# Four low halves of weights from GpSimd to VectorE, and a check of limits as six separate steps

## Chip, cores and metric

One core of one Trainium2 chip runs the whole program. The metric is the device time in microseconds (us) of one execution, the median of several runs.

## What is computed

The reference is a gated linear attention over 4 x 8 heads of 768 steps, followed by a mixture of eight experts with the best two chosen for each token, followed by a dense MLP:

```python
for t in range(S):                                   # attention
    state = alpha[:, :, t, :, None] * state + einsum('bhd,bhe->bhde', k[:, :, t], v[:, :, t])
    y[:, :, t] = einsum('bhd,bhde->bhe', q[:, :, t], state)
x = y.transpose(0, 2, 1, 3).reshape(3072, 384)
z = x @ w_gate + log1p(exp(x @ w_noise)) * noise     # 3072 x 8
top2 = two largest of z per row; weights = softmax of the two
out[tokens of e] += weight * (maximum(x[tokens of e] @ w1[e], 0) @ w2[e])      # 384 -> 1024 -> 384
h = out @ w_in;  result = maximum(0.01 * h, h) @ w_out                         # 384 -> 2048 -> 384
```

## The kernel before

Attention runs in 24 units of 128 tokens (build_unit). The tokens of four units form a tile; for each tile a chain of small VectorE operations (gate_top2 and build_route) picks the two experts and gives every choice a slot, and GpSimd scatters the rows into slots in DRAM with an indirect DMA (L1267, 48 scatters in all). Then the experts run (build_experts): each group is one expert's rows, 320 to 512 of them, and for each 128 of the 1024 hidden columns, a step, there is a first product of 9 matmuls into the PSUM tile ph (gemm1, L751), the high half hh on ScalarE (L769), the low half on VectorE into the same tile (L779), and a second product into py (gemm2, L799 and L795). There are two ph buffers, so a first product waits for the VectorE low half of two steps before. The second product of a step stands two steps behind (LAG = 2). Expert 0's first 320 rows are the first group, begun as the last attention units finish.

Products are made of high and low halves, three matmuls for one. Weights come in pairs of 128-column blocks, four pairs per expert, so pair j serves steps 2j and 2j+1. For each pair w1 and w2 are loaded into staging tiles w1s and w2s (two buffers each, L495 and L498), ScalarE writes the high half (split_hi, L504), and split_lo (L508) subtracts it from the staged tile to give the low half, 128 x 768, after which the staging tile is free for the next load. For expert 0 all eight low halves are on GpSimd, for expert 1 on VectorE, for the others on either.

The order on each engine is written by a planner (class Planner) when the program is built: every step has an estimated duration, what it depends on, rings of buffers, and a due time worked back from those who need it. Among the steps that can start first on an engine, it takes the one with the earliest due time. Steps marked port=True on VectorE and GpSimd are planned one after another. The engines then run their lists in that order, whatever the real times. Scatters are planned at least 1.7 us apart.

The slots were laid out with fixed sizes, so raise_flag checks, once the counts are known, that no limit was broken; if one was, a general path recomputes everything at the end. flag_sums puts the 19 sums on all partitions with small matmuls into the PSUM tile pA, and raise_flag, a single step of the plan with 3.0 us, compares them on VectorE in 18 small instructions (L635 to L652), several of which multiply one SBUF column by another.

Of the kernel before, what the change touches and what calls it, by code (L numbers as in the profile page):

```python
# [7 lines left out]
FT = mybir.dt.float32  # L8
# [5 lines left out]
OP = mybir.AluOpType  # L14
AX = mybir.AxisListType
# [11 lines left out]
SIZES = ((320, 512),) + ((384, 448),) * 7  # L27
G0 = 384
EARLY = 2
# [6 lines left out]
CAP = sum(SIZES[0])  # L36
SURE, CLEARED = 656, 4
# [4 lines left out]
BIG = 1.0e30  # L42
# [38 lines left out]
class Planner:  # L81
# [8 lines left out]
    def add(self, eng, dur, fn, deps=(), use=(), takes=(), phase=1, due=1e9, lat=0.0, size=0, own=1e9, port=False, room=None, rows=0):  # L90

        deps = list(deps)
        st = Step(eng, dur, fn, deps, list(takes), phase, due, lat, size)
        st.port, st.room, st.rows = port, room, rows
        st.own = own
        for owner, ring in use:
            deps.append(owner)
            owner.holders[ring].append(st)
        for ring in st.takes:
            ring.planned.append(st)  # L100
        self.steps.append(st)
        return st
# [271 lines left out]
def tile_kernel(  # L374
# [21 lines left out]
    nc = tc.nc  # L396
    B, H, S, D = q.shape
    N, Dm = B * S, H * D
    E, _, F = w1.shape
# [11 lines left out]
    consts = ctx.enter_context(tc.tile_pool(name="consts", bufs=1))  # L411
# [13 lines left out]
    rt = fctx.enter_context(tc.tile_pool(name="route", bufs=2))  # L425
# [28 lines left out]
    sq = consts.tile([PP, NCH], FT)  # L454
    tots = consts.tile([PP, NCH, HP], FT)
    flag = consts.tile([128, 1], I32)
    m_all, pk_all = (consts.tile([128, 2, NCH], FT, name=nm) for nm in ("m_all", "pk_all"))

    msk = {}

    def route_consts():
        nc.gpsimd.iota(desc, pattern=[[1, E]], base=1, channel_multiplier=0, allow_small_or_imprecise_dtypes=True)
        nc.gpsimd.memset(ones_f, float(E))
        for i in range(2):
            nc.gpsimd.tensor_copy(turn_w[:, :, i * D:(i + 1) * D],
                                  identf[:, None, 64 * i:64 * i + D].to_broadcast([128, HP, D]))
        nc.gpsimd.affine_select(out=tri, in_=ones_f, pattern=[[1, 128]], compare_op=OP.is_gt, fill=0.0,
                                base=0, channel_multiplier=-1)
        nc.gpsimd.memset(ones_b, float(E))
        nc.gpsimd.memset(zeros, 0.0)  # L470
        nc.gpsimd.memset(acc, 0.0)
        nc.gpsimd.tensor_scalar(acc[0:1, 0, :], desc[0:1, :], 1.0 / E, None, op0=OP.mult)
        for n in sorted({NG * len(g) for g in RGROUPS}):
            msk[n] = consts.tile([128, E, n], BF, name=f"msk{n}")
            nc.gpsimd.memset(msk[n], 1.0)
            nc.gpsimd.memset(msk[n][:, :, 0:1], 0.0)
# [3 lines left out]
    PAIRS = [("a", e, j) for e in range(E) for j in range(NP)] + [("b", 0, j) for j in range(F2 // 256)]  # L480
# [20 lines left out]
    def split_hi(i, which):  # L501
        if which == 0:
            alloc_pair(i)
        nc.scalar.activation(WT[i][2 * which], RAW[i, which], AF.Copy)  # L504
# [106 lines left out]
    flags = {}  # L611
# [18 lines left out]
        pe.last = nc.tensor.matmul(pf[:, E:E + 1], ones_f[:PP, :], vm, start=True, stop=True)  # L630

    def raise_flag():
        pf = flags["pf"]
        cm = rt.tile([128, 1], FT, name="cmx")
        nc.vector.tensor_reduce(cm, pf[:, 0:E], axis=AX.X, op=OP.max)  # L635
        nc.vector.tensor_scalar(cm, cm, float(E * CAP + E), None, op0=OP.is_le)
        vs = rt.tile([128, 1], FT, name="vs")
        nc.vector.tensor_scalar(vs, pf[:, E:E + 1], 0.0, None, op0=OP.is_le)
        nc.vector.tensor_mul(vs, vs, cm)
        nc.vector.tensor_reduce(cm, pf[:, 0:E], axis=AX.X, op=OP.add)  # L640
        nc.vector.tensor_scalar(cm, cm, float(E * 2 * N + E * (E + 1) // 2), None, op0=OP.is_equal)
        nc.vector.tensor_mul(vs, vs, cm)
        nc.vector.tensor_reduce(cm, pf[:, 0:E], axis=AX.X, op=OP.min)
        nc.vector.tensor_scalar(cm, cm, float(E * SURE), None, op0=OP.is_gt)
        nc.vector.tensor_mul(vs, vs, cm)
        nc.vector.tensor_reduce(cm, pf[:, E + 1 + EARLY:], axis=AX.X, op=OP.max)
        nc.vector.tensor_scalar(cm, cm, float(E * SURE + E), None, op0=OP.is_le)
        nc.vector.tensor_mul(vs, vs, cm)
        for e in range(EARLY):
            nc.vector.tensor_scalar(cm, pf[:, E + 1 + e:E + 2 + e], float(E * SIZES[e][0]), None, op0=OP.is_ge)  # L650
            nc.vector.tensor_mul(vs, vs, cm)
        nc.vector.tensor_scalar(flag, vs, -1.0, 1.0, op0=OP.mult, op1=OP.add)  # L652


    groups = [("a", e, g) for g in range(2) for e in range(EARLY)]
# [4 lines left out]
    def build_experts(t0, R, scat, cleared_at, ready_at, totals, acc_done, begun):  # L660

        add = plan.add
# [27 lines left out]
        def expert_weights(i, after):  # L690
            e = PAIRS[i][1]
            prev = [WO[i - 1]] if i else []
            phase = 1 if e == 0 else 2
            AUX[i] = []
            for m, nm in enumerate(("w1s", "w2s")):
                fe = add("s", 0.45, lambda m=m: fetch(i, m), after, takes=[R[nm]], size=0.39)
                hi = add("a", 0.73, lambda m=m: split_hi(i, m), prev, use=[(fe, R[nm])] + ([(WO[i], R["W"])] if m else []),
                         takes=[] if m else [R["W"]], phase=phase)
                if m == 0:
                    WO[i] = hi  # L700
                on = "g" if e == 0 else "v" if e < EARLY else "vg"
                AUX[i].append([hi, add(on, dict(v=0.87, g=1.8) if len(on) > 1 else dict(v=0.87, g=1.8)[on],
                                       lambda en=on[0], m=m: split_lo(i, m, en), [hi],
                                       use=[(fe, R[nm]), (WO[i], R["W"])], phase=phase, port=True)])
# [128 lines left out]
        def combine(g, j, kk):  # L833
# [4 lines left out]
            else:  # L838
                nc.vector.scalar_tensor_tensor(ya, YG["b", g, j, 1], wts[:, c, 1:2], ya, op0=OP.mult, op1=OP.add)
                xg_t["b", 0, g, j] = ya  # L840

        out_rows = {0: [], 1: []}
        xdone, S1, S2 = {}, {}, {}
        t = t0
# [48 lines left out]
        tm = [t0]  # L893
# [3 lines left out]
        for si, (gi, f, nf) in enumerate(steps):  # L897
            key = groups[gi]
            if f == 0 and key[0] == "a" and key[2] == (1 if key[1] < EARLY else 0) and EARLY <= key[1] + 1 < E:
                for j in range(NP):  # L900
                    expert_weights((key[1] + 1) * NP + j, [S1[si - 1]["g1"]])
            if gi == 2 * E - 2 and f == 0:
                for j in range(F2 // 256):
                    last_weights(E * NP + j)
            if f == nf - 1 and gi + 1 < len(groups):
                group_in(gi + 1)
                tm[0] += 0.34 * len(blocks(groups[gi + 1]))
            n = sum(b[1] for b in blocks(key))
            dur = 9 * (0.008 + 0.0004375 * n)
            tm[0] += dur  # L910
            i = pair(key, f)
            g1 = add("p", dur, lambda si=si: gemm1(si), flat_list(AUX[i][0]) + xdone[gi] + ([S1[si - 1]["g1"]] if si else []),
                     use=[(XO[key], R["XT"]), (WO[i], R["W"])], takes=[R["ph"]], phase=2, due=tm[0])
            S1[si] = dict(g1=g1)
            k = n / 384
            if key[0] == "a":
                hh = add("a", 0.08 + 0.41 * k, lambda si=si: hidden(si, "hh"), use=[(g1, R["ph"])], takes=[R["hh"]], phase=2)
                hl = add("v", 0.12 + 0.45 * k + (0.12 if n % 128 else 0.0), lambda si=si: hidden(si, "hl"), use=[(g1, R["ph"]), (hh, R["hh"])], phase=2)
            else:
                hc = add("a", 0.5, lambda si=si: hidden(si, "hc"), use=[(g1, R["ph"])], takes=[R["hc"]], phase=2)  # L920
                lk = add("v", 0.6, lambda si=si: hidden(si, "leak"), use=[(hc, R["hc"])], phase=2)
                hh = add("v", 0.47, lambda si=si: hidden(si, "hh"), [lk], use=[(hc, R["hc"])], takes=[R["hh"]], phase=2)
                hl = add("v", 0.63, lambda si=si: hidden(si, "hl"), use=[(hc, R["hc"]), (hh, R["hh"])], phase=2)
            S1[si].update(hh=hh, hl=hl)
            if si >= LAG:
                second(si - LAG)
            if si == first[2 * EARLY]:
                v0 = add("v", 1.3, violations, totals + [S1[first[EARLY]]["g1"]], phase=2, due=tm[0] + 40)
                v1 = add("p", 0.5, flag_sums, [v0] + acc_done, takes=[R["pA"]], phase=2, due=tm[0] + 50)
                add("v", 3.0, raise_flag, use=[(v1, R["pA"])], phase=2, due=tm[0] + 60)  # L930
        for si in range(len(steps) - LAG, len(steps)):
            second(si)

# [1 line left out]
    with ExitStack() as actx:  # L935
# [32 lines left out]
        add = plan.add  # L968
# [595 lines left out]
```

## Time and profile before

| | us |
|---|---|
| median of 3 runs | 1033.15 |
| the three runs | 1034.31, 1033.15, 1027.29 |
| profiled execution | 1029.27 |
| its span | 1027.6 |
| TensorE (PE) busy | 1005.4 (98%) |
| VectorE (DVE) busy | 567.5 (55%) |
| ScalarE (ACT) busy | 384.3 (37%) |
| GpSimd (POOL) busy | 277.6 (27%) |

The span is from the first to the last instruction; 1.67 us of the profiled execution lie around it. The shares are means over very different stages: VectorE is busy throughout in attention (first 140 us or so), TensorE in the experts and the MLP. PEld is TensorE's weight load, SPq the queue that issues DMAs.

### The profile page before, as it was taken

To read this page: it belongs to the slowest core of one execution; us is meant where nothing else is said; L and a number is where in the kernel's file an instruction comes from. 1 tells how busy PE (TensorE), PEld (TensorE's weight loads), DVE (VectorE), ACT (ScalarE), POOL (GpSimd) and SP (SyncE) were. 2 spreads that over 40 slices of the span, in tenths; PEclk is the share of its full clock that TensorE was granted. 3 is DMA by queue.
4 is the path that set the end of the run, shared out by engine and by line. 5 is a ranking of instruction groups with operands and counts; after the bars stand their busy time and mean duration, and the time that the engine had idled before them with its cause. 6 is when DMAs were issued, how large, how long until landed. Compare 5 with 4: busy or idle time off the path is not lost.

```text
span 1027.6 us, 17907 instructions
## 1 busy us (share of the span) xinstructions
PE 1005.4 (98%) x6714; PEld 968.6 (94%) x6714; DVE 567.5 (55%) x1270; ACT 384.3 (37%) x815; POOL 277.6 (27%) x310
## 2 busy tenths in 40 slices
PE   8999889999999999999999999999999999999997
PEld 7888779999899999999999999999999999999997
DVE  8999946224745545454543456645454545454543
ACT  5667535223534545353533342313131313121211
POOL 4377776001122324242322244302020202000000
PEclk9999999999999999999999999999999999999999
DMA  9979737325533646454667564302020202010000
GB/s 256 248 251 292 253 136 241 117 89 177 188 113 133 211 141 206 143 182 155 190 215 260 180 210 136 95 1 70 1 70 1 70 1 70 1 40 1 24 1 27
DMA packets 79507, 133.37 MB, mean 130 GB/s; under 512 B 8498, under 2 KB 57140, under 8 KB 79412
## 3 DMA queue, kind: packets, MB, share of 16 engines
q1 hardware_dynamic: 73268, 113.26, 34.9%
q0 software_dynamic: 6144, 18.88, 5.5%
q8 instruction: 55, 0.90, 0.4%
q14 instruction: 40, 0.33, 0.1%
HBM read 92.98 MB, written 39.13 MB: 129 GB/s over the span
## 4 chain that ended last, share of the span: by engine, by line
PE 85%; DVE 7%; DMA 3%; POOL 2%; issue 2%; ACT 1%; SPq 0%; POOLq 0%; DVEq 0%; ACTq 0%
PE ph L751 40%; PE py L799 38%; PE py L795 2%; DVE pT L1016 2%; DVE pF L1009 2%; PE pA L600 1%; DMA at<-in_al_l_dram 1%; PE pB L600 1%; POOL x_s L1267 1%; DVE kt L1030 1%; DVE qp L1036 1%; DMA kq<-in_kq_l_dram 1%; DMA x_s<-xg,si 1%; POOL w1lA L508 1%; PE pA L1161 1%
## 5 line engine op out<-in xcount | busy, mean ns | idle before, releaser
L799 PE MATMUL py<-w2hA,hh 128*128 128x384 f32 x768 | 220.0, 340 | 0.0
L799 PE MATMUL py<-w2hB,hh 128*128 128x384 f32 x768 | 218.7, 338 | 0.0
L779 DVE SCALAR_TENSOR_TENSOR hh<-ph,hh 128x64 fp32r<-128x64 f32 (+2 forms) x192 | 79.4, 442 | 182.7 <-ACT hh L769 182.6
L761 ACT ACTIVATE hc<-ph 128x384 f32<-128x384 f32 x128 | 62.9, 491 | 283.2 <-PE ph L751 283.2
L764 DVE SCALAR_TENSOR_TENSOR hc<-hc 128x384 f32<-128x384 f32 x128 | 72.4, 565 | 168.7 <-ACT hc L761 168.4
L769 ACT ACTIVATE hh<-ph 128x384 fp32r<-128x384 f32 (+3 forms) x128 | 66.3, 518 | 233.6 <-PE ph L751 207.5
L799 PEld LDWEIGHTS py<-w2hA,hh 128*128 128x128 f32 x768 | 141.5, 189 | 0.9
L799 PEld LDWEIGHTS py<-w2hB,hh 128*128 128x128 f32 x768 | 140.9, 188 | 0.7
L751 PE MATMUL ph<-xh,w1hA 128*128 128x384 f32 (+3 forms) x384 | 134.7, 351 | 4.6 <-DVE hh L779 2.8
L751 PE MATMUL ph<-xh,w1lA 128*128 128x384 f32 (+3 forms) x384 | 132.9, 346 | 0.3 <-POOL w1lA L508 0.3
L751 PE MATMUL ph<-xh,w1hB 128*128 128x384 f32 (+1 forms) x384 | 132.7, 346 | 0.0
L751 PE MATMUL ph<-xl,w1hB 128*128 128x384 f32 (+1 forms) x384 | 132.5, 345 | 0.1
L751 PE MATMUL ph<-xl,w1hA 128*128 128x384 f32 (+3 forms) x384 | 132.4, 345 | 0.0
L751 PE MATMUL ph<-xh,w1lB 128*128 128x384 f32 (+1 forms) x384 | 132.3, 344 | 0.0
L799 PE MATMUL py<-w2lA,hh 128*128 128x384 f32 x384 | 130.0, 339 | 0.3 <-POOL w2lA L508 0.3
L799 PE MATMUL py<-w2lB,hh 128*128 128x384 f32 x384 | 128.7, 335 | 0.0
L830 POOL DMA_INDIRECT xg<-y_d,gidx x48 | 49.5, 1031 | 248.0 <-PE pA L600 117.7
L751 PEld LDWEIGHTS ph<-xh,w1hA 128*128 128x128 f32 x384 | 72.4, 189 | 7.0 <-DVE hh L779 2.1
L751 PEld LDWEIGHTS ph<-xh,w1lA 128*128 128x128 f32 x384 | 72.4, 189 | 3.0 <-POOL w1lA L508 0.6
L782 DVE TENSOR_TENSOR hh<-hc,hh 128x384 fp32r<-128x384 f32 x128 | 72.5, 566 | 4.4
L751 PEld LDWEIGHTS ph<-xl,w1hA 128*128 128x128 f32 x384 | 72.4, 189 | 1.5
L751 PEld LDWEIGHTS ph<-xh,w1lB 128*128 128x128 f32 x384 | 72.1, 188 | 1.7
(181 smaller groups left out, 1572.4 us busy)
## 6 DMA issues: line engine op xcount, KB each, us to landing
w1s<-in_moe_w_dram SPq DMA_DIRECT2D x32, 384.0 KB
w2s<-in_moe_w_dram SPq DMA_DIRECT2D x32, 384.0 KB
kq<-in_kq_l_dram SPq DMA_DIRECT2D x24, 448.0 KB
xg<-x_s SPq DMA_DIRECT2D x48, 192.0 KB
y_d<-ys SPq DMA_DIRECT2D x48, 192.0 KB
nv<-in_v_l_dram SPq DMA_DIRECT2D x24, 256.0 KB
w1s<-in_moe_w_in_dram SPq DMA_DIRECT2D x24, 256.0 KB
w2s<-in_moe_w_out_dram SPq DMA_DIRECT2D x16, 384.0 KB
```

The costliest lines, as they stand in the source:

```text
L600: pe.last = nc.tensor.transpose(p[:, d, :n], src[:n, d * 128:(d + 1) * 128], identf[:n, :n])
L751: pe.last = nc.tensor.matmul(ps[:, :n], a[:, d, fo:fo + 128], x[:, d, :n], start=i == 0, stop=i == len(seq) - 1)
L761: nc.scalar.activation(hc[:, :n], ps[:, :n], AF.Copy)
L764: nc.vector.scalar_tensor_tensor(hc[:, :n], hc[:, :n], 0.01, hc[:, :n], op0=OP.mult, op1=OP.max)
L769: nc.scalar.activation(hh[:, :n], ps[:, :n], AF.Relu)
L779: nc.vector.scalar_tensor_tensor(dst, ps[:, a:b], 0.0, hh[:, a:b].bitcast(FT), op0=OP.max, op1=OP.subtract)
L782: nc.vector.tensor_sub(hl[:, :n], HT[si, "hc"][:, :n], hh[:, :n].bitcast(FT))
L795: pe.last = nc.tensor.matmul(py, HT[si, "both"][:, o:o + 128], w[:, f % 2, :], start=(f == 0 and i == 0), stop=(f == nf - 1 and i == 1))
L799: pe.last = nc.tensor.matmul(py[:n, :], h[:, o:o + n], w[:, f % 2, :], start=(f == 0 and i == 0), stop=(f == nf - 1 and i == 2))
L830: return nc.gpsimd.indirect_dma_start(out=yg, out_offset=None, in_=y_d[0:rows, :], in_offset=bass.IndirectOffsetOnAxis(ap=gidx[:, c, kk:kk ...
L1009: nc.vector.tensor_tensor_scan(rev(suf_f[:, 0:NW - 1]), rev(d["at"][:, 1:NW]), rev(heads_f[:, 1:NW]), 1.0, OP.mult, OP.add)
L1016: nc.vector.tensor_tensor_scan(wt, d["at"][:, i * half:(i + 1) * half], heads_f[:, i * half:(i + 1) * half], 0.0, OP.mult, OP.add)
```

## The change

Two edits. The low halves of expert 0's pairs 2 and 3 (two tiles each, four instructions) go to VectorE, with a planned duration of 0.87 in place of 1.8; those of pairs 0 and 1 stay on GpSimd. And raise_flag is written anew: two tables of 19 columns, roof and base_, hold upper and lower limits; two comparisons of all sums with them, the total of the first eight, its comparison, the number of violations and the flag make six instructions, each a step of its own in the plan (0.17 each). The tables are filled by eight memsets on GpSimd in route_consts.

```diff
+    roof, base_ = (consts.tile([128, 2 * E + 1 + EARLY], FT, name=nm) for nm in ("roof", "base_"))
...
+        nc.gpsimd.memset(roof, BIG)
+        nc.gpsimd.memset(base_, -BIG)
+        nc.gpsimd.memset(roof[:, 0:E], float(E * CAP + E))
+        nc.gpsimd.memset(base_[:, 0:E], float(E * SURE + 1))
+        nc.gpsimd.memset(roof[:, E:E + 1], 0.0)
+        for e in range(EARLY):
+            nc.gpsimd.memset(base_[:, E + 1 + e:E + 2 + e], float(E * SIZES[e][0]))
+        nc.gpsimd.memset(roof[:, E + 1 + EARLY:], float(E * SURE + E))
...
     def raise_flag():
-        pf = flags["pf"]
-        cm = rt.tile([128, 1], FT, name="cmx")
-        nc.vector.tensor_reduce(cm, pf[:, 0:E], axis=AX.X, op=OP.max)
-        nc.vector.tensor_scalar(cm, cm, float(E * CAP + E), None, op0=OP.is_le)
-        vs = rt.tile([128, 1], FT, name="vs")
-        nc.vector.tensor_scalar(vs, pf[:, E:E + 1], 0.0, None, op0=OP.is_le)
-        nc.vector.tensor_mul(vs, vs, cm)
...
-        nc.vector.tensor_scalar(flag, vs, -1.0, 1.0, op0=OP.mult, op1=OP.add)
+        pf, n = flags["pf"], 2 * E + 1 + EARLY
+        bad = rt.tile([128, 2 * n + 1], FT, name="bad", bufs=1)
+        total = rt.tile([128, 2], FT, name="vs")
...
+            nc.vector.tensor_tensor(bad[:, 0:n], pf, roof, op=OP.is_gt)
...
+            nc.vector.tensor_tensor(bad[:, n:2 * n], pf, base_, op=OP.is_lt)
...
+            nc.vector.tensor_reduce(total[:, 0:1], pf[:, 0:E], axis=AX.X, op=OP.add)
...
+            nc.vector.tensor_scalar(bad[:, 2 * n:], total[:, 0:1], float(E * 2 * N + E * (E + 1) // 2), None, op0=OP.not_equal)
...
+            nc.vector.tensor_reduce(total[:, 1:2], bad, axis=AX.X, op=OP.add)
...
+            nc.vector.tensor_scalar(flag, total[:, 1:2], 0.0, None, op0=OP.is_gt)
...
+        return [above, below, summed, missing, counted, raised]
...
-                on = "g" if e == 0 else "v" if e < EARLY else "vg"
+                on = "g" if e == 0 and PAIRS[i][2] < 2 else "v" if e < EARLY else "vg"
...
-                add("v", 3.0, raise_flag, use=[(v1, R["pA"])], phase=2, due=tm[0] + 60)
+                fo = add("v", 0.0, lambda: parts.extend(raise_flag()), [v1], phase=2, due=tm[0] + 60)
+                for k in range(6):
+                    fo = add("v", 0.17, lambda k=k: parts[k](), [fo], use=[(v1, R["pA"])] if k < 3 else [], phase=2,
+                             due=tm[0] + 60 + k)
```

## Rows read from the trace of the kernel before

**Rows 1.** Waits of PE, whole trace: us in total, times, longest.

```profile
PE ph L751 <- DVE hh L779: 2.8, 2, 1.8
...
PE py L799 <- POOL w2lA L508: 0.3, 1, 0.3
PE ph L751 <- POOL w1lA L508: 0.3, 1, 0.3
```

**Rows 2.** Windows: stretch, length, busy of each engine (instructions), PEclk, DMA share, GB/s.

```profile
136.00:146.00 10.00, 7.32 (x57) 6.69 (x57) 5.18 (x14) 5.13 (x11) 8.95 (x7) 0.95 0.48 153
146.00:150.00 4.00, 3.15 (x13) 2.83 (x11) 3.79 (x9) 1.17 (x2) 2.84 (x3) 0.70 0.70 252
...
163.00:264.00 101.00, 101.00 (x559) 96.00 (x557) 43.37 (x77) 37.55 (x66) 15.63 (x12) 1.00 0.46 147
```

**Rows 3.** Timeline at the start of the experts, PE: start, length, [idle before <- releaser].

```profile
144.66 0.38 PE L751 MATMUL ph<-xh,w1hA 128*128 128x320 f32 x1 [1.84 <-ACT hh L769]
...
150.10 0.39 PE L751 MATMUL ph<-xh,w1hA 128*128 128x320 f32 x1 [0.95 <-DVE hh L779]
...
159.58 0.41 PE L751 MATMUL ph<-xh,w1lA 128*128 128x320 f32 x1 [0.31 <-POOL w1lA L508]
...
161.36 0.44 PE L799 MATMUL py<-w2lA,hh 128*128 128x384 f32 x1 [0.32 <-POOL w2lA L508]
```

**Rows 4.** Timeline of PE near 270 us.

```profile
269.45 0.34 PE L799 MATMUL py<-w2hB,hh 128*128 128x384 f32 x1
271.59 0.44 PE L751 MATMUL ph<-xh,w1hA 128*128 128x384 f32 x1 [1.80 <-DVE hh L779]
```

**Rows 5.** Timeline of DVE, 141 to 150 us.

```profile
141.47 2.58 DVE L240 SCALAR_TENSOR_TENSOR g_um<-g_u,g_ex 128x32 f32<-128x32 f32 x1
...
145.77 2.58 DVE L302 SCALAR_TENSOR_TENSOR g_rest<-g_oh,g_z 128x32 f32<-128x32 f32 x1
...
149.41 1.01 DVE L779 SCALAR_TENSOR_TENSOR hh<-ph,hh 128x64 fp32r<-128x64 f32 x4
```

**Rows 6.** Timeline of POOL, same stretch: low halves of expert 0.

```profile
142.15 1.84 POOL L508 TENSOR_TENSOR w2lA<-w2s,w2hA 128x768 fp32r<-128x768 f32 x1
...
146.43 1.85 POOL L508 TENSOR_TENSOR w1lA<-w1s,w1hA 128x768 fp32r<-128x768 f32 x1
...
150.44 1.87 POOL L508 TENSOR_TENSOR w2lA<-w2s,w2hA 128x768 fp32r<-128x768 f32 x1
```

**Rows 7.** Timeline of DVE around the check of limits.

```profile
264.64 0.17 DVE L635 TENSOR_REDUCE cmx<-pA 128x1 f32<-128x8 f32 x1 [0.66 <-PE pA L630]
...
265.68 1.87 DVE L642 TENSOR_TENSOR vs<-vs,cmx 128x1 f32<-128x1 f32 x1
267.58 0.17 DVE L643 TENSOR_REDUCE cmx<-pA 128x1 f32<-128x8 f32 x1
...
267.97 1.56 DVE L645 TENSOR_TENSOR vs<-vs,cmx 128x1 f32<-128x1 f32 x1
...
270.99 1.01 DVE L779 SCALAR_TENSOR_TENSOR hh<-ph,hh 128x384 fp32r<-128x384 f32 x2
```

**Rows 8.** Timeline of POOL there.

```profile
265.67 3.84 POOL L508 TENSOR_TENSOR w1lB<-w1s,w1hB 128x768 fp32r<-128x768 f32 x2 [26.49 <-DVE cmx L641]
```

**Rows 9.** Timeline of ACT there.

```profile
264.37 0.49 ACT L769 ACTIVATE hh<-ph 128x384 fp32r<-128x384 f32 x1 [1.52 <-issue]
```

**Rows 10.** Timeline of POOL at the start: a memset of route_consts, and the work after them.

```profile
4.05 0.12 POOL L476 MEMSET msk<- 128x8 bf16 x1
9.60 1.24 POOL L1080 TENSOR_SCALAR_AFFINE_SELECT am<-ar 128x512 f32<-128x512 f32 x2 [5.43 <-ACT ar L1075]
```

**Rows 11.** Instructions of L508: count, duration in ns min/median/max, first and last start.

```profile
L508 POOL TENSOR_TENSOR w1lA<-w1s,w1hA x9: 1829/1847/1944, 137.4 to 506.9; 128x768 fp32r<-128x768 f32 x9
...
L508 DVE TENSOR_TENSOR w1lA<-w1s,w1hA x7: 951/959/2032, 230.1 to 492.3; 128x768 fp32r<-128x768 f32 x7
```

**Rows 12.** Timeline of ACT: the high half of pair 1's w2.

```profile
96.14 0.85 ACT L504 ACTIVATE w2hA<-w2s 128x768 fp32r<-128x768 f32 x1 [0.67 <-DMA w2s<-in_moe_w_dram]
```

More of the change, by code (lines that the diff above doesn't have):

```diff
@@ L632, in raise_flag, with above, below, summed @@
     def raise_flag():
-        pf = flags["pf"]
-        cm = rt.tile([128, 1], FT, name="cmx")
-        nc.vector.tensor_reduce(cm, pf[:, 0:E], axis=AX.X, op=OP.max)
-        nc.vector.tensor_scalar(cm, cm, float(E * CAP + E), None, op0=OP.is_le)
-        vs = rt.tile([128, 1], FT, name="vs")
-        nc.vector.tensor_scalar(vs, pf[:, E:E + 1], 0.0, None, op0=OP.is_le)
-        nc.vector.tensor_mul(vs, vs, cm)
[L640 to L651, printed above, removed]
-        nc.vector.tensor_scalar(flag, vs, -1.0, 1.0, op0=OP.mult, op1=OP.add)
+        pf, n = flags["pf"], 2 * E + 1 + EARLY
+        bad = rt.tile([128, 2 * n + 1], FT, name="bad", bufs=1)
+        total = rt.tile([128, 2], FT, name="vs")
+        def above():
+            nc.vector.tensor_tensor(bad[:, 0:n], pf, roof, op=OP.is_gt)
+        def below():
+            nc.vector.tensor_tensor(bad[:, n:2 * n], pf, base_, op=OP.is_lt)
+        def summed():
+            nc.vector.tensor_reduce(total[:, 0:1], pf[:, 0:E], axis=AX.X, op=OP.add)
+        def missing():
+            nc.vector.tensor_scalar(bad[:, 2 * n:], total[:, 0:1], float(E * 2 * N + E * (E + 1) // 2), None, op0=OP.not_equal)
+        def counted():
+            nc.vector.tensor_reduce(total[:, 1:2], bad, axis=AX.X, op=OP.add)
+        def raised():
+            nc.vector.tensor_scalar(flag, total[:, 1:2], 0.0, None, op0=OP.is_gt)
+        return [above, below, summed, missing, counted, raised]
     groups = [("a", e, g) for g in range(2) for e in range(EARLY)]
@@ L840, in combine @@
                 xg_t["b", 0, g, j] = ya
+        parts = []
         out_rows = {0: [], 1: []}
```

## The prediction

> **What bounds the kernel now.** I read the list of what TensorE (PE) waited for first, because its busy share of 98% leaves only a few places to gain anything. After the attention stage the list holds little [rows 1]: 2.8 us in two waits for VectorE's low half hh, and 0.3 us each for the GpSimd low halves w1lA and w2lA. The windows say where these can lie: from 163 to 264 us PE was busy for 101.00 of 101.00 us [rows 2]. So a change to another engine is worth what it takes out of PE's few gaps, and everything behind a gap moves up by as much.
>
> The timeline of PE then gives each gap its place. At the start of the experts they are 1.84 us before 144.66, 0.95 before 150.10, 0.31 before 159.58 and 0.32 before 161.36 [rows 3]. The clock also fell there: the mean granted clock is 0.95 from 136 to 146 us and 0.70 from 146 to 150, a spell at the lower level (1.2 of 2.4 GHz) behind the long gap, which cost 0.05 x 10 + 0.30 x 4 = 1.7 us of full-speed time [rows 2]. Much later there is one more gap, 1.80 us before 271.59, released by VectorE [rows 4].
>
> Next the engines that PE waited for. Two small VectorE operations of the routing chain, L240 and L302, took 2.58 us each [rows 5]. They ended at 144.05 and 148.35, just behind GpSimd's splits that ended at 143.99 and 148.28 [rows 6]: each was held until GpSimd was through. Behind them stand the low halves hh that free PE's ph tiles. That is the first two gaps. The next two are the splits themselves, pair 3's w1 and pair 2's w2, which GpSimd did late between its scatters. At 265 us the pattern returns inside the check: L642 and L645, one SBUF column times another, took 1.87 and 1.56 us while GpSimd ran two splits from 265.67 to 269.51, so the check lasted from 264.64 to about 271 and two low halves hh had to stand behind it until 270.99 [rows 7, 8].
>
> **The change part by part.**
>
> *The check.* It removes 18 instructions and adds six. Their price: from L635 to L642 six instructions were begun in 1.04 us [rows 7], 0.17 each, so six are about 1.1 us, and 1.6 if every one has to wait a little for the one before. Two columns in SBUF are no longer combined: the two comparisons read pA in PSUM and one table, the rest reads one operand. What such an instruction does while GpSimd splits is seen at L643: begun at 267.58, in the middle of the split, it took 0.17 us [rows 7, 8]. So I take no stall. Also, the six are separate steps, and the planner may put a low half hh between them. The high half was done at 264.86 [rows 9], and PE needs the ph tile only when its last py matmul has streamed, at about 269.6 [rows 4]. Even with all six ahead, the low half is done by 264.64 + 1.6 + 0.6 = 266.8, almost 3 us in time. What is late next is nothing in the rows: PE had full work before and behind. So this wait goes entirely: -1.80 us, with 0 as the other end, if it is caught as before.
>
> The Trainium skill, State Buffer (SBUF), "Who interferes with whom", has the rule behind this: VectorE and GpSimd share one pair of SBUF ports, a VectorE instruction with two SBUF inputs contends with a GpSimd instruction that reads SBUF, the loser waits for the whole of the other, and one with at most one SBUF input outside the two-port modes does not contend. L642 against L643 agrees (1.87 us against 0.17). The same rule speaks against the first edit, since the moved splits have two SBUF inputs; what that would do is the second rival.
>
> The eight memsets on GpSimd cost about 8 x 0.12 = 1 us, from a small memset at 4.05; the next GpSimd work, at 9.60, came after 5.43 us of idle waiting for ScalarE [rows 10]. That hides them five times over: 0. They would cost their 1 us if that wait were gone.
>
> *The moved splits.* A split is 1.85 us on GpSimd and 0.96 on VectorE at the median [rows 11]. GpSimd loses 4 x 1.85 = 7.4 us, VectorE gains 4 x 0.96 = 3.8. Each split moved also lets the staging tile go, so SP's loads of pairs 4 and 5 are issued earlier; PE was full from 163 us on, so that is worth 0. The scatters behind GpSimd's splits move up too, also for nothing, as PE is already full when the groups that need the last of them come up.
>
> The two direct waits for GpSimd, 0.31 and 0.32 us, go, as VectorE can split these tiles as soon as their high halves are there, ahead of the scatters: -0.63, other end 0.
>
> The 0.95 us before 150.10 is open. It hangs on the hh at 149.41, that is on L302 and on what else VectorE is given before that hh. If GpSimd has no split at 146.43, L302 is not held for 2.4 us, and the gap goes even with one split of 0.96 in front: -0.95. But the split of pair 1's w2, begun at 150.44, had its high half at 97 us [rows 6, 12] and can move into the free place and hold L302 exactly as before. Then VectorE's new splits, pairs 2 and 3 of w1, come on top if they are planned ahead of that hh: 0.96 or 1.92 us later. And a VectorE split can be held itself: the longest took 2.03 us against 0.96 [rows 11], 1.07 more, or 2.1 for two. So the ends are -0.95 and +4.0. The rows nearest to it give both signs for alike reasons, and I take 0.
>
> The gap before 144.66 and the low clock behind it come from the split of pair 0, which is not moved: 0, other end -1.84 - 1.7 = -3.5, if the new order spares L240.
>
> The sum is -1.80 - 0.63 = -2.43 us. Against the profiled execution (span 1027.6, 1029.27 in all) it gives 1026.8. That execution lies 3.9 us below the median of the runs, whose own spread is 7 us, so I carry the sum to the median: 1033.15 - 2.43 = 1030.7 us.
>
> **The rivals.**
>
> First, the start of the experts comes loose. With less split work on GpSimd the routing chain is held neither at L240 nor at L302, and both gaps and the low clock go as well: -2.43 - 0.95 - 3.5 = -6.9, or 1026.3 us. For it speaks that the clock fell only behind the long gap [rows 2, 3]; against it that the split which holds L240 stays where it is.
>
> Second, slower: VectorE's two splits of w1 stand before the hh that frees ph for 150.10, L302 is held by pair 1's split, and the new splits are each held by GpSimd too. PE waits 1.92 + 2.1 = 4.0 us longer, and after a gap as long as that before 144.66 it runs at the lower clock again, another 1.7: +5.7 - 2.43 = +3.3, or 1036.4 us. It decides from the point where that hh comes over 2.43 us later than it did. For it: L240 and L302 show that the planner's estimates leave such holds out. Against it: four of them have to coincide. It is what the skill's rule above comes to if VectorE's splits lose each time.
>
> Third, the check frees nothing, because the planner puts other VectorE work with two SBUF operands around it and hh is held by that: only -0.63, or 1032.5 us. Against it stands the 3 us of room.
>
> Fourth, the new order of steps opens a gap somewhere in the remaining 750 us, as VectorE and GpSimd share out later splits differently. PE had none there, so there is no row to price it; each gap before cost 0.3 to 1.8 us.
>
> **How the numbers follow.** The forecast has 0.55, the loose start 0.12, slower at the start 0.17, no gain in the check 0.08, a new gap elsewhere 0.08. The predicted time is 1030.7 us. A measurement of this kernel can tell about 1% (10 us) from no change, since the three runs differ by 7 us without any. None of the cases reaches 10 us, so within 1% has 0.91; faster by more has 0.04 (the loose start, measured from a low base), slower by more 0.05 (the slow rival with further gaps). The range runs from 1023.0, between the loose start counted from the profiled execution (1029.27 - 6.9 = 1022.4) and from the median, to 1036.5, the slow rival counted from the median.
>
> **What would show it.** In the changed profile PE's wait of 1.80 us near 270 is gone, the six instructions of the check take 0.15 to 0.25 us each beside a GpSimd split, and no wait of PE for GpSimd's w1lA or w2lA is left. On VectorE four splits of expert 0 stand between 144 and 160 us, and the wait before PE's fourth first product (at 150.10 before) is within 1 us of the old one. I am wrong if that wait grows past 3 us, if the low clock lasts longer than before or is gone, or if PE waits at a place that the list of before doesn't have.

## The result and the profile after

The kernel after took 1021.47 us at the median of six runs (1019.51 to 1022.81), against 1034.54 us for six runs of the kernel before, three of them those of the table (1027.29 to 1037.35). The ratio is 0.988, with a 95% interval of 0.984 to 0.991: 13 us less, where 2.4 were forecast, and below the whole range of 1023.0 to 1036.5. A repetition in a later set of runs gave 0.991 (0.988 to 0.993), so the gain is some 10 to 13 us. The profiled execution took 1020.72 us with a span of 1019.0 (before: 1029.27 and 1027.6). The lines of the code have moved: L508 is now L517, L751 is L763, L769 is L781, L779 is L791, L795 is L807, L799 is L811, L1227 is L1243, L1267 is L1283.

The list of PE's waits (us in total, times, longest). Behind the attention stage the list of before had, besides the three lines of [rows 1], one for ScalarE's hh, the wait that ended at 144.66:

```profile
PE ph L751 <- ACT hh L769: 1.8, 1, 1.8
```

In the kernel after only this last one is left:

```profile
PE ph L763 <- ACT hh L781: 1.8, 1, 1.8
PE pM L978 <- POOL hm L437: 1.4, 1, 1.4
```

The second line, like all others of that list, lies in the attention stage. In the timeline of PE the wait is this one; no wait of over 0.25 us follows it to the end:

```profile
143.03 0.38 PE L763 MATMUL ph<-xh,w1hA 128*128 128x320 f32 x1 [1.84 <-ACT hh L781]
```

The windows that answer to [rows 2], and two long stretches late in the kernel. The low clock is where it was and as dear: (1 - 0.92) x 10 + (1 - 0.78) x 4 = 1.7 us:

```profile
136.00:146.00 10.00, 7.32 (x45) 6.91 (x45) 6.38 (x21) 5.14 (x12) 8.13 (x6) 0.92 0.61 199
146.00:150.00 4.00, 4.00 (x21) 4.00 (x21) 1.91 (x6) 0.83 (x2) 2.86 (x2) 0.78 0.57 191
163.00:264.00 101.00, 101.00 (x561) 96.11 (x560) 40.36 (x70) 36.98 (x66) 9.65 (x7) 1.00 0.44 141
...
300.00:600.00 300.00, 300.00 (x1694) 291.91 (x1693) 148.84 (x330) 132.09 (x282) 96.94 (x90) 1.00 0.57 185
620.00:1000.00 380.00, 380.00 (x2204) 379.46 (x2203) 198.65 (x400) 89.33 (x182) 44.90 (x44) 1.00 0.12 38
```

The last two rows hold a surprise. PE is full in both, as it was before, but it gets through more matmuls. The same windows of the kernel before:

```profile
300.00:600.00 300.00, 300.00 (x1685) 290.78 (x1685) 146.27 (x325) 130.64 (x278) 95.03 (x88) 1.00 0.56 181
620.00:1000.00 380.00, 380.00 (x2197) 379.51 (x2196) 200.03 (x402) 89.06 (x182) 45.52 (x45) 1.00 0.12 39
```

Nine matmuls of about 0.177 us and seven of about 0.173 are 2.8 us that come from no wait at all: the mean matmul is a little quicker. The windows hold slightly different pieces of the program, so two fixed points measure it better: from the first matmul of 448 columns to the last matmul of all, before takes 795.03 us (225.99 to 1021.02) and after 790.27 (221.87 to 1012.14). Of the 4.76 us between them 1.80 are the wait before 271.59, and 2.96 come from no wait. It shows best where 27 matmuls of 448 columns follow each other. The first and the last of them in PE's timeline before:

```profile
476.92 0.36 PE L751 MATMUL ph<-xh,w1hB 128*128 128x448 f32 x1
...
482.29 0.37 PE L751 MATMUL ph<-xh,w1lB 128*128 128x448 f32 x1
```

and after:

```profile
469.90 0.36 PE L763 MATMUL ph<-xh,w1hB 128*128 128x448 f32 x1
...
475.17 0.36 PE L763 MATMUL ph<-xh,w1lB 128*128 128x448 f32 x1
```

That is 5.37 us for 26 steps, 206.5 ns each, against 5.27 us, 202.7 ns. Over all starts in the trace from 165 to 1010 us the mean step behind a matmul of 448 columns is 205.9 ns before and 203.1 after (504 of them), of 512 columns 231.1 and 229.2 (72), of 384 columns 176.25 and 175.9 (about 4000): 1.4 + 0.1 + 1.4 = 2.9 us.

VectorE at the start of the experts, which answers to [rows 5]. L240 is held as before, L302 is not, and the moved splits (L517) are not held either:

```profile
139.84 2.58 DVE L240 SCALAR_TENSOR_TENSOR g_um<-g_u,g_ex 128x32 f32<-128x32 f32 x1
...
144.14 0.19 DVE L302 SCALAR_TENSOR_TENSOR g_rest<-g_oh,g_z 128x32 f32<-128x32 f32 x1
...
145.85 0.95 DVE L517 TENSOR_TENSOR w1lA<-w1s,w1hA 128x768 fp32r<-128x768 f32 x1
```

GpSimd in the same stretch, which answers to [rows 6]. The place of pair 2's first split, between the scatters at 143.82 and 146.89, is empty, and pair 1's second split has not moved into it. It stands in the queue behind a scatter that waits 2.10 us for PE:

```profile
140.53 1.82 POOL L517 TENSOR_TENSOR w2lA<-w2s,w2hA 128x768 fp32r<-128x768 f32 x1
...
143.82 0.97 POOL L1283 DMA_INDIRECT x_s<-xg,si  x1 [0.30 <-issue]
146.89 0.97 POOL L1283 DMA_INDIRECT x_s<-xg,si  x1 [2.10 <-PE py L811]
147.87 1.89 POOL L517 TENSOR_TENSOR w2lA<-w2s,w2hA 128x768 fp32r<-128x768 f32 x1
```

The check on VectorE, which answers to [rows 7]; GpSimd ran one split from 263.69 to 265.60. A low half hh has gone between the first two operations, and two splits between the fourth and the fifth:

```profile
263.91 0.18 DVE L647 TENSOR_TENSOR bad<-pA,roof 128x19 f32<-128x19 f32 x1
264.17 0.56 DVE L791 SCALAR_TENSOR_TENSOR hh<-ph,hh 128x384 fp32r<-128x384 f32 x1
264.64 0.17 DVE L650 TENSOR_TENSOR bad<-pA,base__114 128x19 f32<-128x19 f32 x1
...
265.00 2.29 DVE L517 TENSOR_TENSOR w2lB<-w2s,w2hB 128x768 fp32r<-128x768 f32 x2
267.21 0.18 DVE L659 TENSOR_REDUCE vs<-bad 128x1 f32<-128x39 f32 x1
```

### The profile page after: what moved, and what is told of

The parts are those of the page before. It is cut to its first block, busy times and chain, and to the rows that moved or that the text cites. A ratio compares the mean times of both kernels' runs of the same rounds, so it can differ in the third digit from the quotient of the medians.

```text
span 1019.0 us, 17902 instructions
## 1 busy us (share of the span) xinstructions
PE 1001.9 (98%) x6714; PEld 968.3 (95%) x6714; DVE 564.5 (55%) x1263; ACT 384.2 (38%) x815; POOL 268.7 (26%) x313
## 4 chain that ended last, share of the span: by engine, by line
PE 87%; DVE 6%; DMA 2%; issue 1%; ACT 1%; POOL 1%; SPq 0%; POOLq 0%; DVEq 0%; ACTq 0%
PE ph L763 41%; PE py L811 39%; PE py L807 2%; DVE pF L1025 2%; DVE pT L1032 2%; PE pA L609 1%; PE pB L609 1%; DMA at<-in_al_l_dram 1%; DVE kt L1046 1%; DVE qp L1052 1%; DMA x_s<-xg,si 1%; PE pA L1177 1%; PE pY L1147 1%; PE pY L1154 0%; POOL x_s L1283 0%
## 5 line engine op out<-in xcount | busy, mean ns | idle before, releaser
L811 PE MATMUL py<-w2hB,hh 128*128 128x384 f32 x768 | 219.7, 339 | 0.0
L811 PE MATMUL py<-w2hA,hh 128*128 128x384 f32 x768 | 219.4, 339 | 0.0
L791 DVE SCALAR_TENSOR_TENSOR hh<-ph,hh 128x64 fp32r<-128x64 f32 (+2 forms) x192 | 79.6, 443 | 182.7 <-ACT hh L781 181.9
L781 ACT ACTIVATE hh<-ph 128x384 fp32r<-128x384 f32 (+3 forms) x128 | 66.3, 518 | 230.4 <-PE ph L763 201.8
L811 PEld LDWEIGHTS py<-w2hA,hh 128*128 128x128 f32 x768 | 141.1, 189 | 0.8
L811 PEld LDWEIGHTS py<-w2hB,hh 128*128 128x128 f32 x768 | 141.2, 188 | 0.6
L763 PE MATMUL ph<-xh,w1hA 128*128 128x384 f32 (+3 forms) x384 | 134.0, 349 | 1.8 <-ACT hh L781 1.8
L763 PE MATMUL ph<-xh,w1lA 128*128 128x384 f32 (+3 forms) x384 | 132.4, 345 | 0.0
L763 PE MATMUL ph<-xh,w1hB 128*128 128x384 f32 (+1 forms) x384 | 132.0, 344 | 0.0
L763 PE MATMUL ph<-xl,w1hB 128*128 128x384 f32 (+1 forms) x384 | 131.9, 343 | 0.1
L763 PE MATMUL ph<-xl,w1hA 128*128 128x384 f32 (+3 forms) x384 | 131.9, 343 | 0.0
L763 PE MATMUL ph<-xh,w1lB 128*128 128x384 f32 (+1 forms) x384 | 131.8, 343 | 0.0
L811 PE MATMUL py<-w2lA,hh 128*128 128x384 f32 x384 | 129.3, 337 | 0.0
L811 PE MATMUL py<-w2lB,hh 128*128 128x384 f32 x384 | 129.1, 336 | 0.0
L763 PEld LDWEIGHTS ph<-xh,w1hA 128*128 128x128 f32 x384 | 72.3, 188 | 3.3 <-ACT hh L781 2.1
L763 PEld LDWEIGHTS ph<-xh,w1lA 128*128 128x128 f32 x384 | 72.1, 188 | 2.2
L763 PEld LDWEIGHTS ph<-xl,w1hA 128*128 128x128 f32 x384 | 72.3, 188 | 1.3
L763 PEld LDWEIGHTS ph<-xl,w1hB 128*128 128x128 f32 x384 | 72.1, 188 | 1.4 <-DVE xl L618 0.4
```

What stands on the lines that cost most here:

```text
L763: pe.last = nc.tensor.matmul(ps[:, :n], a[:, d, fo:fo + 128], x[:, d, :n], start=i == 0, stop=i == len(seq) - 1)
L781: nc.scalar.activation(hh[:, :n], ps[:, :n], AF.Relu)
L791: nc.vector.scalar_tensor_tensor(dst, ps[:, a:b], 0.0, hh[:, a:b].bitcast(FT), op0=OP.max, op1=OP.subtract)
L811: pe.last = nc.tensor.matmul(py[:n, :], h[:, o:o + n], w[:, f % 2, :], start=(f == 0 and i == 0), stop=(f == nf - 1 and i == 2))
```

## The experiments

The theories that stood at the beginning: A, the difference between the two profiles is the waits that went, about 4 us, and the rest is chance between executions; B, the profiled execution of before was a lucky one, and a usual one waits longer at the start of the experts. When these runs showed the quicker matmuls, C (the pace hangs on where the tiles lie) and D (it comes with the new check's instructions) were added, and H, that one split of the four decides the start. Each set of four kernels, and the last of two, shared its own runs of the kernel before (17 to 23), to which the ratios refer. In the expectations a bias step is a low half hh, and a combine is L240 or L302.

**e1, the kernel before again, and e2, the kernel after again.** No edit.

> The kernel before, unchanged, timed against itself. Theory A (the two edits save only TensorE's gaps, about 2.2 us at the start of the experts and 1.9 us at the check, and the rest of the 13 us lies between executions or chips): ratio 1.000, and a second profile whose gaps are those of the first (1.84, 0.95, 0.3, 0.3 and 1.8 us) within half a us each; its span may be some us off through the pace of all matmuls and the attention stage. Theory B (a usual execution of the kernel before has longer gaps than the profiled one): ratio 1.000 too, but the profile, if it is one of 1033 us or more, shows gaps at the start of the experts or at the check that are several us longer.

> The changed kernel again, beside the kernel before on one chip. Theory A: about 4 us faster (ratio 0.996), the 13 us of the first measurement having been mostly chips or executions. Theory B: again 11 to 14 us faster (ratio 0.987 to 0.989).

e1 took 1032.21 us (ratio 1.001, 0.999 to 1.003), e2 1021.53 (0.991, 0.988 to 0.993). The profile of e1 is a different one from [rows 3, 5, 6]. First VectorE:

```profile
143.82 2.56 DVE L302 SCALAR_TENSOR_TENSOR g_rest<-g_oh,g_z 128x32 f32<-128x32 f32 x1
...
147.07 2.34 DVE L1227 TENSOR_TENSOR_SCAN run<-msk,ot 128x32 bf16<-128x32 bf16 x1
...
149.56 1.01 DVE L779 SCALAR_TENSOR_TENSOR hh<-ph,hh 128x64 fp32r<-128x64 f32 x4
```

then GpSimd and PE's wait:

```profile
144.49 1.84 POOL L508 TENSOR_TENSOR w1lA<-w1s,w1hA 128x768 fp32r<-128x768 f32 x1
146.49 0.99 POOL L1267 DMA_INDIRECT x_s<-xg,si  x1 [0.17 <-issue]
147.50 1.82 POOL L508 TENSOR_TENSOR w2lA<-w2s,w2hA 128x768 fp32r<-128x768 f32 x1
...
150.25 0.60 PE L751 MATMUL ph<-xh,w1hA 128*128 128x320 f32 x1 [4.60 <-DVE hh L779]
```

and the windows, with the granted clock in the third column from the end:

```profile
146.00:150.00 4.00, 0.00 (x0) 0.00 (x0) 3.79 (x8) 0.25 (x1) 3.14 (x3) 0.95 0.50 169
150.00:165.00 15.00, 14.12 (x70) 13.46 (x71) 4.91 (x19) 3.81 (x8) 6.91 (x5) 0.79 0.39 131
```

Pair 2's split holds L302, the scatter behind it goes at once, pair 1's split follows beside the scan and holds that as well, and PE stands for 4.60 us. Then the clock falls for (1 - 0.95) x 4 + (1 - 0.79) x 15 = 3.4 us. Place and clock cost 8.0 us together, where the first profile of before has 0.95 + 1.7. From the first matmul into ph to the 55th it takes 23.7 us in e1, 18.9 in the first profile of before, 17.7 in the first of after and 16.5 in e2. In the first profile of before the clock had fallen earlier, so that PE was late with the py on which the scatter waits ([rows 2]: 0.70 from 146 to 150 us), and pair 1's split came after the scan. So there are two kinds of executions. The later profiles with the old splits are of the same two: in e5 and e14 the clock fell right behind the wait of 1.84 us (0.94 and 0.95 from 138 to 146 us, 0.93 before), and the next wait was 1.11 and 0.94 us; in e4 and e7, as in e1, it stayed at 1.00 up to the next wait, which was 4.62 us. The times of e1's twelve runs fall in two groups to match: four took 1026.6 to 1028.6 us at a mean granted clock of 0.996 to 0.998, eight took 1031.4 to 1035.2 at 0.993 to 0.995. The 19 runs of before beside them part in the same way; in the other sets the times of before run on without such a gap, so not every run can be put to a kind by its time. B holds. A falls.

**e3, the four splits alone, and e4, the check alone.** e3 is the kernel before with the diff's line `on = "g" if e == 0 and PAIRS[i][2] < 2 else ...`; e4 the kernel after with that line as it was.

> Only the four low halves of expert 0 on VectorE, the check as before. Theory A: 2.2 us faster (ratio 0.998), the gaps before the fourth first product and the waits for GpSimd's w1lA and w2lA gone, the 1.8 us at the check still there. Theory B: either this or the check alone carries 8 us or more; if it is the start of the experts, the ratio here is 0.990.

> Only the new check, the low halves on GpSimd as before. Theory A: 1.9 us faster (ratio 0.998), the 1.8 us gap near 270 gone, the start of the experts as before. Theory B: ratio 0.990 here if what varies from execution to execution is the check's holds.

e3 took 1025.51 us (0.994, 0.992 to 0.997), e4 1026.35 (0.994, 0.992 to 0.997): 5.8 us each by their ratios, 11.6 together, where e2 of the same set, with both, shows 9.6 (7.1 to 12.1). In e3 PE waits 1.84 us at the start and 1.80 at the check, and the steps behind 448 columns are 205.9 ns; its six runs lie within 3.1 us. In e4 the check's wait is gone and the steps are 203.1 ns; at the start it has the long form of e1, 4.62 us, and its eight runs spread over 8.8 us. So the pace comes with the check's edit, and the two kinds of executions go with the splits.

**e5, e6 and e7: places.** The built programs show what the check's edit moves (the traces hold no addresses). The tables `roof` and `base_` take 96 bytes of each partition apiece and stand in front of nearly all tiles, and `bad` takes 96 bytes more than the column `cmx` had and stands in front of the gathered rows, hh, the second half of the weights and the second set of turned rows. So these lie 192 or 288 bytes further on. e5 puts the tables, filled and never read, and the size of `bad` into the kernel before; e7 the size of `bad` alone; e6 is the kernel after with its results in a tile that was there:

```
...
e5, e7  -        cm = rt.tile([128, 1], FT, name="cmx")
        +        cm = rt.tile([128, 2 * (2 * E + 1 + EARLY) + 1], FT, name="bad", bufs=1)[:, 0:1]
...
e6      -        bad = rt.tile([128, 2 * n + 1], FT, name="bad", bufs=1)
        +        bad = rt.tile([128, NCH * (HP + 1)], FT, name="ok", bufs=1)[:, 0:2 * n + 1]
...
```

> The kernel before with its old check and its four GpSimd splits; added are only the two tables (filled at the start, read by nobody) and a row of 39 columns in the place of the check's one-column tile, so that every later tile lies where it lies in the kernel after (192 bytes further behind the tables, 288 bytes further behind the row). Theory C (the matmuls' pace hangs on where their tiles lie): 448-column matmuls start every 203.1 ns as in after and in the kernel with the new check alone, not every 205.9 ns; the stretch from 300 us to the end is about 2.5 us shorter, the whole 2.9 us (ratio 0.997); the waits at the start and at the check stay as in before (4 to 5 us, 1.2 to 1.8 us). Theory D (the pace comes with the new check's instructions): 205.9 ns, time as before (1.000).

> The kernel after with its row of results put into a tile that was there before, so that every tile behind the tables moves by the same 192 bytes and none by 288. If what counts is how the later tiles lie against the earlier ones (theory C in the form that bad's odd 96 bytes do it): 448 columns every 205.9 ns again, 2.9 us above the kernel after (1024.4), waits as in after. If any shift does it (the tables' 192 bytes alone): 203.1 ns and 1021.5. Theory D (instructions of the check): 203.1 ns and 1021.5 too, so this run is read together with the one before and the one behind it.

> The kernel before with the check's one-column tile made 39 columns wide and nothing else: all behind it moves by 96 bytes, no instruction changes. Theory C with the 96 bytes: 203.1 ns per 448 columns, time 2.9 us below before (0.997). Theory C with the tables' 192 bytes, or theory D: 205.9 ns, 1.000. Waits at start and check as in before.

e5 took 1029.49 us (0.997, 0.994 to 0.999), e7 1028.81 (0.995, 0.993 to 0.998), e6 1025.58 (0.991, 0.989 to 0.994). The steps behind 448 columns are 203.1 ns in e5, 203.15 in e7 and 205.8 in e6. The windows of e7, in which not one instruction differs from before:

```profile
300.00:600.00 300.00, 300.00 (x1691) 291.86 (x1690) 146.48 (x326) 131.96 (x282) 95.22 (x88) 1.00 0.56 181
620.00:1000.00 380.00, 380.00 (x2205) 379.52 (x2204) 201.35 (x406) 89.72 (x183) 46.48 (x45) 1.00 0.13 39
```

and of e6, which runs all of the new instructions:

```profile
300.00:600.00 300.00, 300.00 (x1689) 290.92 (x1687) 148.14 (x329) 132.74 (x283) 97.06 (x90) 1.00 0.57 184
620.00:1000.00 380.00, 380.00 (x2197) 379.50 (x2196) 199.13 (x400) 89.00 (x182) 45.38 (x44) 1.00 0.12 38
```

C holds and D falls, and what does it is `bad`'s odd 96 bytes, not the tables' 192. Of 2.9 us expected, the ratios show 3.6 for e5 and 4.7 for e7, with 2.9 in both intervals. The waits are the old ones: e5 has 1.83, 1.11, 0.31, 0.34 and 1.77 us, e7 has 4.62 at the start. In e5 the clock fell behind the wait at the check as well (0.68 from 270 to 274 us, 0.90 from 274 to 278), another 1.7 us.

**e8, pair 0's second split on VectorE too.** The line reads `... PAIRS[i][2] < 2 and (PAIRS[i][2], m) != (0, 1) ...`.

> The kernel after with pair 0's second low half on VectorE too. Theory: the wait of 1.84 us that is left before 143 us is the combine (2.58 us instead of 0.2) held by that split on GpSimd; with the split on VectorE (0.95 us) it goes, and the low clock of 3.41 us behind it with it: 1.8 to 3.5 us below the kernel after (1018 to 1019.7). Rival: the split runs ahead of the combine or of the bias step on VectorE and delays it by its 0.95 us, so that half of the wait stays: 1020.5. The order written ahead of it in the attention shifts by one matmul group, for which I allow 2 us to either side.

1023.87 us in four runs (0.990, 0.988 to 0.993): no gain over the kernel after. L240 is free (0.19 us), but the planner now puts the low half hh behind the whole routing chain, and PE waits longer than the 1.84 us of the kernel after:

```profile
142.09 0.19 DVE L240 SCALAR_TENSOR_TENSOR g_um<-g_u,g_ex 128x32 f32<-128x32 f32 x1
...
145.09 1.02 DVE L791 SCALAR_TENSOR_TENSOR hh<-ph,hh 128x64 fp32r<-128x64 f32 x4
...
145.79 0.38 PE L763 MATMUL ph<-xh,w1hA 128*128 128x320 f32 x1 [2.48 <-DVE hh L791]
```

**e9 and e10: which of the four splits.** e9 is the kernel after with only pair 2's first split on VectorE, e10 its counterpart with the other three. The conditions are `(PAIRS[i][2], m) != (2, 0)` and `(PAIRS[i][2] < 2 or (PAIRS[i][2], m) == (2, 0))`.

> The kernel after with only one of the four splits on VectorE (pair 2's first low half, the one that stood between the second and the third scatter on GpSimd's queue); pair 2's second and both of pair 3's are back on GpSimd. Theory H (that one split holds the combine L302, and by delaying TensorE lets pair 1's second split start beside the scan and hold that too): no wait at the start but the 1.84 us, combine and scan at 0.2 us each; only the two direct waits of 0.3 us each on GpSimd's late splits may come back: within 1 us of after (1021.5 to 1023). Rival (each split on GpSimd in this stretch costs its share of the 6 us): three quarters of the gain gone, about 1026, with waits of some us between 150 and 165 us.

> The counterpart: the kernel after with pair 2's first low half back on GpSimd and the other three on VectorE. Theory H: the combine L302 takes about 2.5 us, in most executions the scan is held too, the wait before the fourth first product is 1 to 4.6 us with 1.7 to 6.8 us of low clock, so the median lies 4 to 5 us above after (about 1026, as with the new check alone) and the runs spread over 6 us or more. Rival (each split its share): 1.5 us above after (1023), runs within 3 us.

e9 took 1025.63 us (0.996, 0.994 to 0.998), e10 1024.44 (0.996, 0.994 to 0.998), against 1022.33 and 1021.24 for the two kernels of the same set that have all four on VectorE (e11, e12). H is half right. In e9 L302 and the scan are free (0.19 and 0.23 us) and the runs lie within 3.9 us, as H says; but the three splits that remain on GpSimd now follow each other, and a conversion begun at 153.41 is held through all three. VectorE, GpSimd and PE's wait:

```profile
153.41 5.78 DVE L1273 CAST si<-pk_all 128x8 uint32<-128x8 f32 x1 [0.18 <-DVE pk_all L1269]
...
152.77 0.97 POOL L1283 DMA_INDIRECT x_s<-xg,si  x1 [0.30 <-issue]
153.76 1.86 POOL L517 TENSOR_TENSOR w1lA<-w1s,w1hA 128x768 fp32r<-128x768 f32 x1
155.56 3.60 POOL L517 TENSOR_TENSOR w2lA<-w2s,w2hA 128x768 fp32r<-128x768 f32 x2
...
159.79 0.38 PE L763 MATMUL ph<-xh,w1hA 128*128 128x320 f32 x1 [3.06 <-DVE hh L791]
```

In e10 L302 is held (2.58 us), PE waits 1.29 us at 149.01, and the runs spread from 1021.9 to 1031.2 us, as H says; but the median is only 2 to 3 us above the versions with all four moved, where H said 4 to 5. So the wide spread comes with pair 2's first split, and the other three have to go with it because on GpSimd they would hold something else.

**e11, the six operations as one step.** The planner gets one step that issues all six, where it had six that others may pass.

```
...
-                for k in range(6):
-                    fo = add("v", 0.17, lambda k=k: parts[k](), [fo], use=..., due=tm[0] + 60 + k)
+                add("v", 1.0, lambda: [part() for part in raise_flag()], use=[(v1, R["pA"])], ...)
...
```

> The kernel after with its six operations of the check issued as one step, one behind the other, where after lets the order put bias steps between them. If it is the number and the kind of the operations that frees the path: at 0.15 to 0.25 us each the six take 1.0 to 1.5 us, the bias step behind them is at most some 0.5 us late, wait near 270 us under 0.5 us, time as after (1021.5). If it is the splitting into steps: the bias step waits for all six, one of them held by GpSimd's split to 2 us, and a wait of 1.2 to 1.8 us is back (1023).

1022.33 us (0.993, 0.990 to 0.995), with no wait near 270 us. The six took 0.15 to 0.19 us each, from 264.94 to 265.89, while GpSimd ran a split from 264.72 to 266.63. The split and the longest of the six:

```profile
264.72 1.91 POOL L517 TENSOR_TENSOR w1lB<-w1s,w1hB 128x768 fp32r<-128x768 f32 x1 [28.74 <-ACT w1hB L513]
...
265.50 0.19 DVE L659 TENSOR_REDUCE vs<-bad 128x1 f32<-128x39 f32 x1
```

**e12, all big tiles 32 bytes further on**, so that all begin at a multiple of 64 bytes; in the kernel after all begin at 32 above one, in the kernel before some at 0 and some at 32.

> The kernel after with one unused tile of 32 bytes a partition in front of all its big tiles, so that weights, turned rows and hidden tiles all begin at a multiple of 64 bytes, where in after all begin at 32 above one and in before some at 0 and some at 32. If only the places of operands against each other count: pace and time as after (203.1 ns, 1021.5). If a start at a multiple of 64 is better in itself: 448 columns below 203 ns, 1 to 3 us less; if worse: above.

1021.24 us (0.992, 0.990 to 0.994) and 203.2 ns behind 448 columns: as the kernel after. In every version at the quick pace the second set of tiles lies 96 bytes further from the first than in the kernel before, in every one at the slow pace (before, e3, e6, e14) it does not. So what counts, as far as these runs go, is how the tiles lie to each other.

**e13, all low halves of expert 0 to whichever engine is free**: `on = "vg" if e == 0 else ...`. **e14, the old eighteen operations as eighteen steps**, splits and tiles as before.

> The kernel after with all eight low halves of expert 0 left to whichever of VectorE and GpSimd the planner finds free, which puts none on GpSimd in the start of the experts; the order has the first bias step right behind the combine L240 this time, then one split of 0.95 us, then the routing chain. Theory H (a combine begun beside a scatter that is followed at once by a split is held until the split ends): L240 takes 0.2 us, the wait of 1.84 us before 143 us and the low clock behind it go: 1.8 to 3.5 us below after (1018 to 1019.7). Rival (the splits that VectorE takes over come in front of bias steps or the routing chain and cost as much): time as after (1021.5), the wait moves to a later first product, 1 us or more.

> The kernel before with its old eighteen operations of the check issued as eighteen steps of their own, so that bias steps can come between; no tile moves, the splits stay on GpSimd. If the operations' number and kind made the wait near 271 us (held ones of 1.2 to 1.9 us in a row in front of the bias step), the steps alone take it away just as well, since the bias steps may pass: the wait goes, 1.2 to 1.8 us below before (ratio 0.998 to 0.999), pace 205.9 ns, start as in before. If a bias step still finds held operations in front of it: wait of 0.5 to 1.8 us near 271 us, 1.000.

e13 took 1021.41 us (0.989, 0.986 to 0.992), as the kernel after. L240 is free, hh follows it at once, and the wait of 1.84 us is gone with all of the low clock. But a split and the routing chain then stand before the next hh:

```profile
147.75 0.39 PE L763 MATMUL ph<-xh,w1hA 128*128 128x320 f32 x1 [0.93 <-DVE hh L791]
```

From the first matmul into ph to the 55th it took 16.4 us, against 17.7 in the profile of the kernel after and 16.5 in e2 and e12, where the clock did not fall there. So L240 is what held PE for 1.84 us, but freeing it gave nothing over an execution in which the clock stays up: a wait of 0.93 us and the splits in front of hh have taken it back. No version that was run is faster than the kernel after.

e14 took 1030.34 us (0.998, 0.996 to 1.000). The low halves hh do pass between the old operations, but four of these, of two SBUF columns each, are still held (0.72, 1.39, 1.39 and 1.02 us in place of 0.16), and PE waits for the check itself, which keeps the pA tile for the next transposes:

```profile
267.42 1.39 DVE L644 TENSOR_TENSOR vs<-vs,cmx 128x1 f32<-128x1 f32 x1
...
273.04 0.55 PE L600 MATMUL pA<-identf,xg 128*128 128x128 f32 x3 [1.39 <-DVE cmx L642]
```

So it is the kind and number of the operations that frees PE, not the steps. The runs of e14, with the splits as before, again fall in two groups: six from 1027.5 to 1028.8 us, six from 1031.9 to 1034.1.

## Why the prediction was wrong

*The check, -1.80: right.* The wait of 1.80 us (1.21 in e1) is gone in every kernel with the six operations, and it is there in those with the old ones beside GpSimd's splits (1.80 in e3, 1.77 in e5). The six take 0.15 to 0.19 us each beside a split (e11), as L643 had it. The room of 3 us was there too: e11 loses nothing with all six in a row.

*The memsets, 0: right.* GpSimd did them from 3.88 us on, and its next work, at 10.47, still came after 5.91 us of idle for ScalarE.

*The two direct waits, -0.63: right.* They are in e5 (0.31 and 0.34) and in no kernel with the four splits on VectorE.

*The wait before 144.66 and its clock, 0: right* for the profiled executions, 1.84 us and 1.7 before and after. In e2 and e3 the same wait was followed by no low clock there. That L240 sets this wait, as the prediction read it, e13 bears out.

*The wait before 150.10, taken as 0: this step failed, in its direction and in its size.* The prediction let the split of pair 1's w2 "move into the free place and hold L302 exactly as before". It did not: GpSimd works its queue in order, and in the order that the planner wrote a scatter stands in front of that split and waits for PE's py, 1.15 us before and 2.10 us after. So the place stayed empty, L302 and the scan ran free, and the wait went entirely: -0.95 against the profiled execution. Against an execution like that of e1 it is -4.60 and -3.4 of low clock; the prediction took its price from one execution of a kernel that has two kinds, and then carried the sum to the median, which belongs to the other kind as far as the groups of e1 tell. The first rival, the start comes loose, had the nearest time and half the mechanism: L302 came loose, L240 did not. The second rival's held splits did not occur in the first profile of the kernel after; e2 has one, of 1.73 us in place of 0.95, without a wait of PE behind it, and e10 one of 2.48. The one of e2:

```profile
151.81 1.73 DVE L517 TENSOR_TENSOR w1lA<-w1s,w1hA 128x768 fp32r<-128x768 f32 x1
```

*A term that was missing, and so stood at nothing: -2.9 us of pace.* The tables and the row of results were costed as instructions only. As tiles they moved everything behind them, and all matmuls of the experts had other places to read from. e5, e6, e7 and e12 show that it is this and nothing else of the edit.

The terms together, from rows: check -1.2 to -1.8; pace -2.9; start -1.6 (0.95 + 0.63) against the lucky kind and some -6 to -8 against the other, by whether the clock falls after the change too. That is -6 to -13, and 1.7 more where the clock falls behind the check's wait as in e5. Against its own profiled execution the span fell by 8.6 us, of which these terms explain 6.3 and an earlier start of the experts 1.6 (the first matmul into ph comes at 138.31 in place of 139.94 us); 0.7 us stay open. That start differs by 1.9 us between the two profiles of before and by 3.2 between those of after, so the 1.6 are not put down to the change. The measured medians say 10 to 13. The parts agree with the whole: places 0.9965 (e5) times the rest 0.9915 (e6) is 0.988.

The Trainium skill, SBUF — State Buffer, section "Who interferes with whom", says that a VectorE instruction with two SBUF inputs contends with a GpSimd instruction that reads SBUF, and that casts can too where their operands allow a mode on two ports. The held ones here, L240, L302, the scan and the conversion, are of these kinds; whether the conversion's operands allow that mode no run shows. It also says that the loser waits for the whole of the other; the 5.78 us of e9 show that it can be three others, one behind the other.

Open: why the clock falls right after the wait of 1.84 us in some executions and not in others, and by what mechanism the places set the pace; the runs show only that they do.

## What to carry to other kernels

Before pricing a gap, look whether the kernel's runs fall in groups, with their granted clocks, and ask which group the profiled execution belongs to; a gap that hangs on a race between two engines has two sizes. Before letting work move into a free place on an in-order queue, read what stands in front of it and what that waits for. And a new small tile in front of big ones is an edit of its own: compare the matmuls' step in full stretches before crediting a gain to the instructions.

## What the runs showed of the hardware that was not expected

- Matmuls of 448 columns start every 205.9 or every 203.1 ns at a full granted clock, by where the tiles in SBUF lie to each other: 96 bytes more in front of one half of them, with no instruction changed, made 2.9 us of 1030 by these steps (e7), and shifts of 192 or 32 bytes that all share changed nothing (e6, e12).
- A small VectorE operation of two SBUF inputs, begun while GpSimd issues a scatter that is followed at once by a split, takes 2.3 to 2.6 us in place of 0.2; begun beside a scatter with no split behind it, it takes 0.19 (L302 at 144.14 in the kernel after). The operations of the check that read the PSUM tile pA took 0.16 to 0.18 us beside a split (e11). A conversion of one SBUF input was held for 5.78 us through three splits.
- An early fall of the clock can be the cheaper case: where it fell right behind the wait of 1.84 us, PE came late, and a scatter and a split came too late to hold the scan (0.95 us of wait and 1.7 of clock against 4.60 and 3.4).
